# Opening of a fused attention and feed-forward kernel: other load order, two weight quarters centred late, query tiles in spare buffers

## The chip, the cores and the metric

The kernel runs on one core of a Trainium2 chip. The metric is device time in microseconds (us) of one execution; lower is better. The kernel before takes 1200.5 us, the median of three runs (1200.47 to 1202.93).

## The reference

Three blocks follow each other on batches of 576 rows (8 batches, 8 heads of 64, 32 memory slots). Everything is float32 on the host; the matrices w_ch1, w_ch2, w_in and w_out arrive as 64-bit floats.

```
a = softmax(phi over the rows);  k_m = a^T k;  v_m = a^T v
x = softmax(q k_m^T / 8) v_m                      # heads side by side: (8, 576, 512)
xn = (x - mean) / sqrt(var + 1e-6) * g_ln
x = x + relu(xn @ w_ch1) @ w_ch2                  # 512 -> 2048 -> 512
h = gelu(x @ w_in); u, v = halves of h
v = layernorm(v) * g_ln2; v = w_sg @ v + b_sg     # mixes the 576 rows
out = x + (u * v) @ w_out
```

## The kernel before, in words

Phase 1 does attention and the first feed-forward block, phase 2 the rest. Two batches make a pair of nine 128-row tiles; the last 64 rows of both batches share the fifth tile.

W1 (w_ch1) is used in four quarters `fb` of 512 columns. Since x is attn times v_m, the kernel multiplies each quarter by v_m first (`make_vw`, product `pvw`, L561), so that the first feed-forward product `ph` (`m1`, L609) takes the attention weights `aTh`, `aTl` directly. The mean that the layer norm subtracts is taken out of W1 instead: `center_w1` forms the column means of a scaled quarter on TensorE (`cm`, L509; for quarters 1 to 3 in L514 and L521) and subtracts them in place on VectorE (L523), and only then does `make_vw` read the quarter. A matrix product is three products of a high and a low part; `evict_vw` casts the high part on ScalarE (L567) and forms the low part on VectorE (L568).

64-bit weights become 32-bit in `to_f32`: one pass on ScalarE (L116) and two on VectorE (L117, L118) per 128x512 piece. `scale_w1` then scales a W1 piece (L501), `split_w2` splits one of the sixteen W2 pieces.

The hidden layer goes in chunks of 128 columns: `m1` makes `ph` (six products) in one of two PSUM buffers, `relu` takes it out as `hh` on ScalarE (L595) and `hl` on VectorE (L596), and three chunks later `m2` multiplies it by W2 into `py` (L639 to L641). So the third chunk in a row cannot begin before the `hl` of the first is done. A block is 256 or 320 rows; for batch 0 two blocks (j0 and j1) take turns, four chunks each per quarter.

The order is set by `at_time(time, function)`: a sorted list of events, emitted between the chunks. A scheduler then orders each engine's instructions; `issue_after` holds an instruction behind a named one. Every engine works through its own queue in order. All loads and stores go through the one queue of SyncE (SP, `load`, L89) in the order in which they stand there.

For batch 0 phi is loaded, its maximum over the rows subtracted (`prep_max`, `prep_exp`), k_m and v_m formed (`prep_kv`), the query tiles turned (`t_q`), and softmaxed (`t_scores`, `t_norm`, `t_attn`) in three groups: two tiles, two tiles, and the 64 remaining rows. From batch 1 on a query tile lies in one buffer (tag `q`), is turned on VectorE (L381), and the next load waits for that.

Of the kernel before, what the change touches and what calls it, by code (L numbers as in the profile page):

```python
# [28 lines left out]
def fused_kernel(ctx: ExitStack, tc: tile.TileContext, q, k, v, phi, g1, w1, w2, w_in, g2, w_sg, b_sg, w_out, out):  # L29
# [36 lines left out]
    make_identity(nc, ident)  # L66
# [39 lines left out]

    def to_f32(raw, gate=None):
# [4 lines left out]
        gates = ExitStack()  # L112
        for ins in gate or ():
            gates.enter_context(tc.issue_after(ins.ins))
        with gates:
            A.activation(hi.bitcast(F32), hi.bitcast(F32), AF.Prelu, scale=2.0 ** -112, alpha=-(2.0 ** 32))  # L116
            V.tensor_scalar(lo, lo, 29, None, op0=ALU.logical_shift_right)  # L117
            V.scalar_tensor_tensor(out=lo, in0=hi, scalar=3, in1=lo, op0=ALU.logical_shift_left, op1=ALU.bitwise_or)  # L118
        return lo.bitcast(F32)
# [27 lines left out]
    def phase1():  # L147
# [10 lines left out]
        VBs = [[at.tile([P, 2, 4 * D], F32R, name=f"VB{n}{i}") for n in "hl"] for i in range(2)]  # L158
        for i in range(2):
            for t in VBs[i]:  # L160
                G.memset(t.bitcast(F32), 0.0)
        prz = at.tile([P, 2, 4, NM], F32, name="prz")
        G.memset(prz, 0.0)
# [66 lines left out]
        def load_q(u, b, i):  # L230
            n = u["n"]
            if b == 0:
                if i % 2 == 0:
                    t = wpool.tile([P, 2, DM], F32, tag="w", name="q0") if i == 4 else tail.tile([P, 2, DM], F32, tag="vw", name="q0", bufs=VTAIL)
                    st["q0"] = t[:, 0, :], t[:, 1, :]
                t = st["q0"][i % 2].rearrange("p (c o d) -> p c o d", c=4, o=2)[:n]
                load(t.rearrange("p c o d -> p (c o) d"), q[b, :, i * P:i * P + n, :].rearrange("h p d -> p h d"))
            else:
                t = at.tile([P, 4 * DM // 16, 4], F32, tag="q", name="q").rearrange("p a b -> p (a b)")[:, 0:4 * n]
                if n == P:  # L240
                    load(t, u["q_d"].rearrange("a (t r) c f -> (a t) (r c f)", t=32))
                else:
                    for a in range(4):
                        load(t[32 * a:32 * a + 32], u["q_d"][a, 0:n].rearrange("(t r) c f -> t (r c f)", t=32))
            u["q"] = t
            u["seen"].add("q")

        def prep_max(b, gs):
            ph, pr = st["phi", b]
            n, hs = len(gs), slice(4 * gs[0], 4 * gs[-1] + 4)  # L250
            p, tag = (at, "kvn") if gs[0] == 0 else (at, "z")
            pm = p.tile([P, H, NM], F32, tag=tag, name="pm")[:, hs]
            with tc.issue_after(st["hl"].ins) if b else ExitStack():
                V.tensor_reduce(out=pm, in_=ph[:, hs].rearrange("p h c m -> p h m c"), axis=AX.X, op=ALU.max)
                for i, g in enumerate(gs):
                    rows, sub = slice(REM * g, REM * g + REM), slice(4 * i, 4 * i + 4)
                    V.tensor_tensor(out=pm[rows, sub], in0=pm[rows, sub], in1=pr[rows, g], op=ALU.max)
# [107 lines left out]
        def t_q(gr, i):  # L365
# [9 lines left out]
            if b == 0:  # L375
                pt = ps_0([P, 4, n], "ptq")
                for c in range(4):
                    PE.transpose(pt[:, c, :], t[:, c].rearrange("p o d -> p (o d)"), ident[:n, :n])
# [11 lines left out]
        def t_scores(gr):  # L390
# [7 lines left out]
            with whole(b):  # L398
                for kT, cs in parts:
                    for j in range(4):  # L400
                        for g in range(2):
                            rs_, ms = slice(64 * g, 64 * g + 64), slice(32 * j, 32 * j + 32)
                            mm = PE.matmul(sc[g][ms, cs], kT[rs_, ms], qT[rs_, j, cs], start=True, stop=True, skip_group_check=True)  # L403
                            for name in claims:
                                tc.add_manual_dep(mm.ins, name, ORDER, reason="all eight parts of the array together")
            nb = 2 * w // 32
# [4 lines left out]
            for g in range(2):  # L411
                V.transpose(out=z[:, g * w:(g + 1) * w], in_=sc[g])
# [3 lines left out]
            V.tensor_tensor(out=z3, in0=z3, in1=m.unsqueeze(2).to_broadcast([P, nb, NM]), op=ALU.subtract)  # L416
            A.activation(z, z, AF.Exp, scale=SCALE)
            gr["z"] = z, z3, nb

        def t_norm(gr):  # L420
            z, z3, nb = gr["z"]
            r = at.tile([P, 16], F32, tag="r0", name="r0")[:, 0:nb]
            V.tensor_reduce(out=r, in_=z3, axis=AX.X, op=ALU.add)
# [4 lines left out]
        def t_attn(gr):  # L428
# [6 lines left out]
            for i, u in enumerate(us):  # L435
# [6 lines left out]
                A.copy(ah, src)  # L442
# [52 lines left out]
        def scale_w1(fb):  # L495

            WC[fb] = ws = wc_tiles()
            for j, raw in enumerate(raws.pop(fb)):
                d = ws[j // 2][:, j % 2, :]
                w = to_f32(raw, [st.get("hl", tiles[TB - 1]["tr"])] if fb else None)  # L500
                last = A.activation(d, w, AF.Copy, scale=g1c[:, j:j + 1])  # L501
            st["scales"] = [last.ins.name]

        def center_w1(fb):
# [5 lines left out]
            else:  # L510
                four = ps_of(fb, [P, DM], "cm4")
                claim = V.memset(four[:, 0:2], 0.0).ins.name
                for j in range(KC):
                    ins = PE.matmul(four[32 * j:32 * j + 32], mean[:, 0:32], ws[j // 2][:, j % 2, :], start=True, stop=True, skip_group_check=True)  # L514
                    tc.add_manual_dep(ins.ins, claim, ORDER, reason="all four parts of the array together")
                    for other in st["scales"]:
                        tc.add_manual_dep(ins.ins, other, ORDER, reason="all four parts of the array together")
                part = at.tile([P, DM], F32, tag="at32", name="part")
# [3 lines left out]
            for n in range(2):  # L522
                V.tensor_tensor(out=ws[n], in0=ws[n], in1=cm.unsqueeze(1).to_broadcast([P, 2, DM]), op=ALU.subtract)  # L523
# [10 lines left out]
        def make_vw(b, turns):  # L534
# [20 lines left out]
            with whole(b):  # L555
                for fb, ps in runs:
                    ws = WC[fb]
                    for j in range(KC):
                        for g in range(HK):
                            rs_, ms = slice(64 * g, 64 * g + 64), slice(32 * j, 32 * j + 32)  # L560
                            mm = PE.matmul(ps[g][ms, :], vT[rs_, ms], ws[j // 2][rs_, j % 2, :], start=True, stop=True, skip_group_check=True)  # L561
                            for n in claims:
                                tc.add_manual_dep(mm.ins, n, ORDER, reason="all eight parts of the array together")

        def evict_vw(b, turn):
            for ps, (h, l) in zip(st.pop(("vw", b, turn)), VW[b, TURNS[b % 2][turn]]):
                A.copy(h, ps)  # L567
                V.tensor_tensor(out=l, in0=ps, in1=h.bitcast(F32), op=ALU.subtract)  # L568
# [5 lines left out]
        def split_w2(c):  # L574

            gate = st.get("hl", tiles[1 if c == 0 else 3]["tr"])
            W2[c] = split([raws.pop(("w2", c))], wpool, gate=[gate])
# [83 lines left out]

        last_q = -99.0
        for b in range(B):
# [17 lines left out]
            at_time(pb - 2 if b == 0 else pb + 0.6 * f, load_rem, b)  # L681
# [32 lines left out]
            for gi, (items, base) in enumerate(zip(groups, bases)):  # L714
# [6 lines left out]
                if b == 0:  # L721
                    for i, (tt, qi, _, ub) in enumerate(items):
                        at_time(-27, load_q, us[i], ub, qi)
                        at_time(-21 + 0.1 * tt, t_q, gr, i)
                        at_time(1.3 + tt + (tt > 1), t_x, gr, i)
                    tt = items[-1][0]
                    at_time(-17 + 0.1 * tt, t_scores, gr)
                    at_time(-16 + 0.1 * tt, t_norm, gr)
                    at_time(-16 + 0.1 * tt, t_attn, gr)
# [5 lines left out]
                for i, (tt, qi, _, ub) in enumerate(items):  # L735
                    at_time(base - early - 2 + 0.5 * i, lay_q, us[i], ub, qi)
                    at_time(max(base - early, last_q + 0.05), load_q, us[i], ub, qi)
# [18 lines left out]
        for fb in range(NFB):  # L756
            at_time((-26.5, -26.2, -2.5, 2.0)[fb], load_w1, fb)
            at_time((-16.5, -5.0, 3.0, 7.5)[fb], scale_w1, fb)
            at_time((-16.4, -0.3, 4.6, 9.1)[fb], center_w1, fb)
            at_time((-15, 1.3, 5.8, 10.3)[fb], make_vw, 0, [fb])  # L760
            at_time((-15, 1.3, 5.8, 10.3)[fb], evict_vw, 0, fb)
            at_time((1.4, 3.0, 7.4, 12.0)[fb], store_w1, fb)
        for c in range(NF):
            split_at = 4.5 * (c // 4) + 0.5625 * (c % 4) - 0.6 if c > 3 else 0.9 * c - 4
# [383 lines left out]
```

## Time and profile before

| what | value |
|---|---|
| median of three runs | 1200.5 us |
| the profiled execution | 1201.19 us |
| its span in the trace | 1199.4 us |
| TensorE busy over the span | 97% |
| granted TensorE clock, mean | 0.991 of full |

TensorE (PE) is the engine to watch: from about 150 us on it has hardly any idle time. In the rows, DVE is VectorE, ACT is ScalarE, POOL is GpSimd, SP is SyncE, and SPq its queue. Times are us from the start of the span; L numbers are lines of the kernel before.

### The profile page before, as it was taken

The numbers are of one execution on the slowest core, as the hardware profiler recorded it, in microseconds if no ns is written. First come the engines' busy times: TensorE is split into PE (matmuls) and PEld (weight loads), VectorE is DVE, ScalarE is ACT, GpSimd is POOL, SyncE is SP. The second block draws the span as 40 slices with busy tenths as digits, with TensorE's granted clock in tenths as the row PEclk, the third lists the DMA queues.
The fourth block names the chain that finished last, engine by engine and source line by source line (L and its number), as shares of the span: only waits on it lengthen the run. The fifth ranks groups of instructions, "written<-read, shape, count | busy, mean of one in ns | idle before, by whom it ended". The sixth has DMA issues, their size and how long they took to land.

```text
span 1199.4 us, 20678 instructions
## 1 busy us (share of the span) xinstructions
PE 1163.3 (97%) x7717; PEld 988.3 (82%) x7717; DVE 685.6 (57%) x1666; ACT 468.6 (39%) x1066; POOL 401.5 (33%) x623
## 2 busy tenths in 40 slices
PE   4799799999999999999999999999999999999998
PEld 3477578888788888788888888889989988998997
DVE  4896655755644646644546455567575376447532
ACT  3764332323432332422333345445444354344430
POOL 2224221311201211201211112557666476566641
PEclk9799999999999999999999999999999999999999
DMA  8984825463341642241410343122340051022201
GB/s 236 377 250 133 216 74 135 112 181 63 97 126 22 162 115 67 88 117 27 120 36 27 107 140 98 36 74 89 89 141 10 19 158 62 1 88 89 71 19 71
DMA packets 198580, 124.14 MB, mean 104 GB/s; under 512 B 92944, under 2 KB 173712, under 8 KB 198480
## 3 DMA queue, kind: packets, MB, share of 16 engines
q1 hardware_dynamic: 198480, 122.82, 35.8%
q8 instruction: 61, 1.00, 0.3%
q14 instruction: 39, 0.32, 0.1%
HBM read 99.72 MB, written 31.33 MB: 109 GB/s over the span
## 4 chain that ended last, share of the span: by engine, by line
PE 87%; DVE 5%; DMA 3%; SPq 2%; ACT 1%; issue 1%; POOL 1%; POOLq 0%; DVEq 0%
PE ph L609 16%; PE py L639 10%; PE py L641 10%; PE py L640 10%; PE pvs L1053 8%; PE po L1076 8%; PE pv L943 8%; PE pu L1028 7%; PE pvw L561 2%; SPq L89 2%; DMA q<-q_d 2%; PE kvp L317 1%; DVE qT L381 1%; PE sc L403 1%; PE px L460 1%
## 5 line engine op out<-in xcount | busy, mean ns | idle before, releaser
L609 PE MATMUL ph<-aTh,vw 128*128 128x320 f32 (+1 forms) x1024 | 248.4, 301 | 6.9 <-DVE hl L596 4.4
L639 PE MATMUL py<-whl,hh 128*128 128x512 f32 x512 | 201.6, 396 | 4.9 <-ACT hh L595 4.8
L609 PEld LDWEIGHTS ph<-aTh,vw 128*128 128x128 f32 x1024 | 178.9, 190 | 32.5 <-DVE hl L596 8.8
L640 PE MATMUL py<-whl,hh 128*128 128x512 f32 x512 | 201.3, 393 | 0.0
L641 PE MATMUL py<-whl,hl 128*128 128x512 f32 x512 | 182.7, 397 | 0.0
L595 ACT ACTIVATE hh<-ph 128x256 fp32r<-128x256 f32 x256 | 96.8, 386 | 168.1 <-PE ph L609 109.6
L596 DVE SCALAR_TENSOR_TENSOR hl<-ph,hh 128x256 fp32r<-128x256 f32 x256 | 106.6, 421 | 89.1 <-ACT hh L595 88.2
L609 PE MATMUL ph<-aTl,vw 128*128 128x256 f32 (+1 forms) x512 | 152.5, 298 | 0.0
L639 PEld LDWEIGHTS py<-whl,hh 128*128 128x128 f32 x512 | 96.3, 188 | 30.9 <-ACT hh L595 8.1
L1053 PE MATMUL pvs<-wsh,vhl 128*128 128x288 f32 x576 | 121.1, 295 | 0.0
L640 PEld LDWEIGHTS py<-whl,hh 128*128 128x128 f32 x512 | 96.5, 188 | 18.5
L1028 PE MATMUL pu<-yTh,whl 128*128 128x288 f32 x512 | 111.0, 295 | 0.2 <-DVE ug L932 0.2
L609 PEld LDWEIGHTS ph<-aTl,vw 128*128 128x128 f32 x512 | 97.4, 190 | 10.8 <-issue 3.3
L641 PEld LDWEIGHTS py<-whl,hl 128*128 128x128 f32 x512 | 90.2, 189 | 11.6 <-issue 2.1
L1053 PEld LDWEIGHTS pvs<-wsh,vhl 128*128 128x128 f32 x576 | 94.3, 188 | 0.8
L943 PE MATMUL pv<-whl,yTh 128*128 128x512 f32 x288 | 90.8, 395 | 0.0
L1076 PE MATMUL po<-whl,gh 128*128 128x512 f32 x288 | 90.2, 392 | 0.0
L1028 PEld LDWEIGHTS pu<-yTh,whl 128*128 128x128 f32 x512 | 85.1, 188 | 1.9 <-DVE ug L932 0.9
L595 ACT ACTIVATE cr<-ph 128x64 fp32r<-128x64 f32 x128 | 28.7, 227 | 123.1 <-PE ph L609 122.4
L1056 POOL TENSOR_TENSOR gt<-gt,ug 128x288 f32<-128x288 f32 x64 | 52.7, 825 | 68.3 <-DVE gt L1055 61.9
L1053 PE MATMUL pvs<-wsl,vhl 128*128 128x288 f32 x256 | 75.5, 295 | 0.0
L1028 PE MATMUL pu<-yTl,whl 128*128 128x288 f32 x256 | 75.5, 295 | 0.0
(165 smaller groups left out, 2148.9 us busy)
## 6 DMA issues: line engine op xcount, KB each, us to landing
raw<-in_moe_w_ch_dram SPq DMA_DIRECT2D x32, 512.0 KB, 7.9
wc<-w_d SPq DMA_DIRECT2D x28, 512.0 KB, 6.0
y_d<-x SPq DMA_DIRECT2D x36, 256.0 KB, 2.5
yt<-y_d SPq DMA_DIRECT2D x36, 256.0 KB, 2.8
yr<-y_d SPq DMA_DIRECT2D x36, 256.0 KB, 2.9
kv<-in_k_dram SPq DMA_DIRECT2D x32, 256.0 KB, 4.0
kv<-in_v_dram SPq DMA_DIRECT2D x32, 256.0 KB, 4.3
out_dram<-yr SPq DMA_DIRECT2D x32, 256.0 KB, 2.0
```

The lines of the kernel that those rows point to most:

```text
L89: return nc.sync.dma_start(out=out_ap, in_=in_ap)
L595: high = A.activation(out_h, src, AF.Relu)
L596: return high, V.scalar_tensor_tensor(out=out_l, in0=src, scalar=0.0, in1=out_h.bitcast(F32), op0=ALU.max, op1=ALU.subtract)
L609: R["ph"] = PE.matmul(ph, w_[:, ks], x[:, g, 0:w], start=(n == 0), stop=(n == 3 * HK - 1))
L639: PE.matmul(py, hh, wh, start=start, stop=False)
L640: PE.matmul(py, hh, wl, start=False, stop=False)
L641: PE.matmul(py, hl, wh, start=False, stop=stop)
L943: PE.matmul(pv, y[:, kc, cs], w, start=(n == 0), stop=(n == 3 * KC - 1))
L1028: PE.matmul(pu, w[:, ds_], y[:, kc, cs], start=(n == 0), stop=(n == 3 * KC - 1))
L1053: PE.matmul(pvs, v_, w_, start=(n == 0), stop=(n == len(ops) - 1))
L1056: G.tensor_tensor(out=gt, in0=gt, in1=ug, op=ALU.mult)
L1076: PE.matmul(po, gg[:, dc, cs], w, start=(n == 0), stop=(n == 3 * KC - 1))
```

## The change

Loads: the zeroing of `prz` (the rest rows of phi) comes first on GpSimd, and its two loads stand right behind phi; the rest rows of k and v come after all of k and v; only the first two query tiles of batch 0 are loaded ahead of W1's first quarter, the other three behind it. Softmax: batch 0's first group is taken through scores, norm and turning before the second. Means: for quarters 0 and 1 `center_w1` only stores the negative means (`ncm`, ScalarE); `make_vw` adds a second product with them to the uncentred one, and the centring in place (`center_late`) follows later, since the stored quarter is read again by later batches. Gates: the conversion of the next quarter and of W2 pieces is held behind the low parts of the last quarter and behind `center_late`. Queries: in batch 1 every second query tile lies in one of the seven `x` buffers.

```diff
-            with tc.issue_after(st["kvT", b][1].ins):
+            with behind([lead["ah"] if b == 0 else st["kvT", b][1]]):
...
-                w = to_f32(raw, [st.get("hl", tiles[TB - 1]["tr"])] if fb else None)
+                w = to_f32(raw, [st["hl"], *lead["quarter"]] if "hl" in st else [lead["ah"], R["word"]] if fb else None)
...
-                part = at.tile([P, DM], F32, tag="at32", name="part")
+                part = at.tile([P, DM], F32, tag="at32" if fb == 3 else "q", name="part")
...
+            if fb < 2:
+                st["cm", fb] = at.tile([P, DM], F32, tag="at32" if fb else "z", name="ncm")
+                A.mul(st["cm", fb], cm, -1.0)
+                lead["quarter"] = lead["scaled"],
+            else:
+                for n in range(2):
+                    centred = V.tensor_tensor(out=ws[n], in0=ws[n], in1=cm.unsqueeze(1).to_broadcast([P, 2, DM]), op=ALU.subtract)
+                lead["quarter"] = lead["scaled"], centred
+
+        def center_late(fb):
+            with behind([st["hl"], *lead["quarter"]]):
+                for ws in WC[fb]:
+                    centred = V.tensor_tensor(out=ws, in0=ws, in1=st["cm", fb].unsqueeze(1).to_broadcast([P, 2, DM]), op=ALU.add)
+            lead["quarter"] = lead["scaled"], centred
...
+                    if late:
+                        for j in range(KC):
+                            for g in range(HK):
+                                rs_, ms = slice(64 * g, 64 * g + 64), slice(32 * j, 32 * j + 32)
+                                PE.matmul(ps[g][ms, :], vT[rs_, ms], st["cm", fb][rs_], start=False, stop=True, skip_group_check=True)
...
+                if b == 1 and i % 2:
+                    t = mo.tile([P, DM], F32, tag="x", name="q", bufs=7)
...
-            at_time((-16.5, -5.0, 3.0, 7.5)[fb], scale_w1, fb)
+            at_time((-17.5, -5.0, 3.0, 7.5)[fb], scale_w1, fb)
...
+            if fb < 2:
+                at_time((1.6, 6.2)[fb], center_late, fb)
```

VectorE's queue around the low parts of quarter 1, before (`vw` is the low part, `hl` the chunk's low part, `s` the layer-norm statistics of a tile):

```order
L568 TENSOR_TENSOR vw<-pvw,vw 128x512 x2
L469 BN_STATS s_697<-x 128x6
L512 MEMSET cm_796 128x2
L470 BN_AGGR mv<-s_697 128x2
L472 TENSOR_SCALAR ve<-mv 128x2
L95 TENSOR_SCALAR rs_t<-ve 128x2
L469 BN_STATS s_917<-x 128x6
L596 SCALAR_TENSOR_TENSOR hl<-ph,hh 128x256
```

The same place now (line numbers are those of the changed kernel; L597 is the low part, L545 `center_late`, L119 and L120 the conversion, L628 `hl`):

```order
L597 TENSOR_TENSOR vw<-pvw,vw 128x512 x2
L545 TENSOR_TENSOR wc<-wc,ncm 128x1024 x2
L119 TENSOR_SCALAR raw_515<-raw_515 128x512
L119 TENSOR_SCALAR raw_517<-raw_517 128x512
L119 TENSOR_SCALAR raw_519<-raw_519 128x512
L119 TENSOR_SCALAR raw_521<-raw_521 128x512
L481 BN_STATS s_713<-x 128x6
L524 MEMSET cm_812 128x2
L628 SCALAR_TENSOR_TENSOR hl<-ph,hh 128x256
```

Two centring passes and four conversion passes have come to stand between the low parts and the first `hl`.

VectorE's queue around the low parts of quarter 2 now (L279 and L282 subtract phi's maximum for batch 1):

```order
L597 TENSOR_TENSOR vw<-pvw,vw 128x512 x2
L545 TENSOR_TENSOR wc<-wc,ncm 128x1024 x2
L119 TENSOR_SCALAR raw_634<-raw_634 128x512
...
L279 TENSOR_TENSOR phi<-phi,mb 128x1024
L282 TENSOR_TENSOR prz<-prz,mb 64x128 x2
L120 SCALAR_TENSOR_TENSOR raw_634<-raw_634 128x512
L120 SCALAR_TENSOR_TENSOR raw_636<-raw_636 128x512
L120 SCALAR_TENSOR_TENSOR raw_638<-raw_638 128x512
L120 SCALAR_TENSOR_TENSOR raw_640<-raw_640 128x512
L628 SCALAR_TENSOR_TENSOR hl<-ph,hh 128x256
```

Before, the low parts of quarter 2 had one conversion pass between them and then only `cr`, L273 and L276 (as L279 and L282 here) ahead of `hl`; the centring of quarter 1 and all four conversions stood earlier.

TensorE's queue at quarter 1's product, before (`py` is the second feed-forward product, here of block j1, `px` the attention output of a tile):

```order
L561 MATMUL pvw<-wc,kvT 32x512 x8
L639 MATMUL py_760<-whl,hh 128x512
L640 MATMUL py_760<-whl,hh 128x512
L639 MATMUL py_764<-whl,hh 128x512
...
L641 MATMUL py_764<-whl,hl 128x512
L609 MATMUL ph<-aTh,vw 128x256
```

The same place now (L592 is the product with the means, L641 is `ph`, L472 `px`):

```order
L673 MATMUL py_780<-whl,hl 128x512
L585 MATMUL pvw<-wc,kvT 32x512 x8
L592 MATMUL pvw<-ncm,kvT 32x512 x8
L641 MATMUL ph<-aTh,vw 128x256
L641 MATMUL ph<-aTl,vw 128x256
L641 MATMUL ph<-aTh,vw 128x256
L641 MATMUL ph<-aTl,vw 128x256
L472 MATMUL px<-VBh_142,aTl 128x4x64
```

The twelve `py` that stood between the product and the first `ph` of the quarter now stand ahead of the product.

## Rows read from the trace of the kernel before

**Rows 1.** The page, part 1: busy us, share, instructions.

```profile
PE 1163.3 (97%) x7717; PEld 988.3 (82%) x7717; DVE 685.6 (57%) x1666; ACT 468.6 (39%) x1066; POOL 401.5 (33%) x623
```

**Rows 2.** Windows: length, engines busy (x), PEclk, DMA share, GB/s.

```profile
31.05:36.30 5.25, 5.24 (x6) 1.80 (x6) 4.83 (x13) 5.15 (x10) 0.40 (x1) 0.54 1.03 415
40.68:47.24 6.56, 3.15 (x16) 2.22 (x16) 6.56 (x20) 3.41 (x8) 0.85 (x1) 0.92 1.00 400
47.24:53.00 5.76, 5.76 (x23) 3.68 (x24) 4.25 (x9) 4.80 (x10) 2.48 (x2) 0.50 0.88 301
53.00:119.00 66.00, 65.25 (x444) 49.95 (x444) 49.05 (x113) 39.69 (x85) 22.14 (x27) 1.00 0.71 211
119.00:155.00 36.00, 28.44 (x200) 20.62 (x200) 22.82 (x62) 12.79 (x34) 7.57 (x10) 0.95 0.84 229
141.70:145.10 3.40, 3.40 (x10) 3.01 (x11) 2.87 (x9) 1.45 (x3) 0.00 (x0) 0.50 0.91 181
```

**Rows 3.** Windows of the loading stretch, for their last column.

```profile
3.00:7.50 4.50, 0.00 (x0) 0.00 (x0) 1.94 (x2) 0.00 (x0) 0.49 (x2) 1.00 1.00 282
7.50:10.50 3.00, 0.41 (x2) 0.28 (x2) 0.57 (x2) 0.00 (x0) 0.00 (x0) 1.00 0.46 101
16.50:21.00 4.50, 4.35 (x44) 2.83 (x38) 1.22 (x5) 1.18 (x3) 1.08 (x3) 1.00 1.10 194
```

**Rows 4.** Timeline of SP's queue: start, us, what.

```profile
3.98 2.91 SPq L89 DMA_DIRECT2D prz<-in_phi_dram  x2
```

**Rows 5.** Timeline of DVE in the opening.

```profile
9.75 0.60 DVE L257 TENSOR_TENSOR pm<-pm,prz 64x128 f32<-64x128 f32 x2 [4.29 <-DMA prz<-in_phi_dram]
```

**Rows 6.** Timeline of ACT in the opening.

```profile
29.13 0.71 ACT L116 ACTIVATE raw<-raw 128x512 f32<-128x512 f32 x1 [0.62 <-DMA raw<-in_moe_w_ch_dram]
```

**Rows 7.** Timeline of PE in the opening.

```profile
31.05 5.24 PE L509 MATMUL cm<-wc,mcol 128*128 128x512 f32 x6 [1.02 <-ACT wc L501]
...
40.68 0.39 PE L609 MATMUL ph<-aTh,vw 128*128 128x256 f32 x1 [0.88 <-ACT vw L567]
...
47.24 0.58 PE L609 MATMUL ph<-aTh,vw 128*128 128x256 f32 x1 [2.91 <-DVE hl L596]
```

**Rows 8.** Lines of DVE, 62 to 93 us: count, busy us, mean ns.

```profile
L118 DVE SCALAR_TENSOR_TENSOR raw<-raw 128x512 uint32<-128x512 uint32 x13 | 8.5, 688 | 0.1
L596 DVE SCALAR_TENSOR_TENSOR hl<-ph,hh 128x256 fp32r<-128x256 f32 x9 | 3.8, 419 | 0.6 <-ACT hh L595 0.4
L117 DVE TENSOR_SCALAR raw<-raw 128x512 uint32<-128x512 uint32 x9 | 3.5, 421 | 0.0
L469 DVE BATCH_NORM_STATS2 s<-x 128x6 f32<-128x512 f32 x4 | 2.8, 692 | 1.6 <-ACT x L463 1.6
L568 DVE TENSOR_TENSOR vw<-pvw,vw 128x512 fp32r<-128x512 f32 x4 | 2.7, 685 | 0.0
L523 DVE TENSOR_TENSOR wc<-wc,cm 128x1024 f32<-128x1024 f32 x2 | 2.4, 1231 | 0.0
L254 DVE TENSOR_REDUCE pm<-phi 128x256 f32<-128x1024 f32 x1 | 2.0, 2043 | 0.0
L273 DVE TENSOR_TENSOR phi<-phi,mb 128x1024 f32<-128x1024 f32 x1 | 1.2, 1222 | 0.4 <-PE mb L272 0.4
```

**Rows 9.** Timeline of PE at quarter 1's product.

```profile
65.06 1.09 PE L561 MATMUL pvw<-wc,kvT 64*32 64x512 f32 x16
...
68.96 0.28 PE L609 MATMUL ph<-aTh,vw 128*128 128x256 f32 x1
...
71.56 0.40 PE L609 MATMUL ph<-aTh,vw 128*128 128x256 f32 x2
```

**Rows 10.** Timeline of PE, batch 1's queries.

```profile
132.71 0.41 PE L609 MATMUL ph<-aTh,vw 128*128 128x320 f32 x1 [1.46 <-DVE hl L596]
...
141.70 0.79 PE L639 MATMUL py<-whl,hh 128*128 128x512 f32 x1 [3.63 <-ACT hh L595]
```

**Rows 11.** Timeline of DVE, the same stretch.

```profile
138.86 1.08 DVE L381 STREAM_TRANSPOSE qT<-q 128x512 f32<-128x512 f32 x1 [4.27 <-DMA q<-q_d]
```

More of the change, by code (lines that the diff above doesn't have):

```diff
@@ L105, in rsqrt_of, with behind @@
         return y
+    def behind(gate):
+        es = ExitStack()
+        for ins in gate or ():
+            es.enter_context(tc.issue_after(ins.ins))
+        return es
     def to_f32(raw, gate=None):
@@ L110, in to_f32 @@
         lo, hi = words[:, :, 0], words[:, :, 1]
[L112 to L115, printed above, removed]
+        with behind(gate):
             A.activation(hi.bitcast(F32), hi.bitcast(F32), AF.Prelu, scale=2.0 ** -112, alpha=-(2.0 ** 32))
             V.tensor_scalar(lo, lo, 29, None, op0=ALU.logical_shift_right)
-            V.scalar_tensor_tensor(out=lo, in0=hi, scalar=3, in1=lo, op0=ALU.logical_shift_left, op1=ALU.bitwise_or)
+            R["word"] = V.scalar_tensor_tensor(out=lo, in0=hi, scalar=3, in1=lo, op0=ALU.logical_shift_left, op1=ALU.bitwise_or)
         return lo.bitcast(F32)
@@ L158, in phase1 @@
         VBs = [[at.tile([P, 2, 4 * D], F32R, name=f"VB{n}{i}") for n in "hl"] for i in range(2)]
+        prz = at.tile([P, 2, 4, NM], F32, name="prz")
+        G.memset(prz, 0.0)
+        make_identity(nc, ident)
         for i in range(2):
@@ L376, in t_q @@
                 pt = ps_0([P, 4, n], "ptq")
-                for c in range(4):
-                    PE.transpose(pt[:, c, :], t[:, c].rearrange("p o d -> p (o d)"), ident[:n, :n])
+                with behind([lead["sc"]] if "sc" in lead else None):
+                    for c in range(4):
+                        PE.transpose(pt[:, c, :], t[:, c].rearrange("p o d -> p (o d)"), ident[:n, :n])
                 A.copy(out, pt)
@@ L410, in t_scores @@
                 z = at.tile([P, 4 * P], F32, tag="z", name="z")[:, 0:2 * w]
-            for g in range(2):
-                V.transpose(out=z[:, g * w:(g + 1) * w], in_=sc[g])
+            with behind([lead["sub"]] if b == 0 and "sub" in lead else None):
+                for g in range(2):
+                    V.transpose(out=z[:, g * w:(g + 1) * w], in_=sc[g])
             z3 = z.rearrange("p (b m) -> p b m", m=NM)
@@ L422, in t_norm @@
             r = at.tile([P, 16], F32, tag="r0", name="r0")[:, 0:nb]
-            V.tensor_reduce(out=r, in_=z3, axis=AX.X, op=ALU.add)
+            with behind(lead.get("evicted") if gr["b"] == 0 and gr["n"] < P else None):
+                V.tensor_reduce(out=r, in_=z3, axis=AX.X, op=ALU.add)
             V.tensor_scalar(r, r, 1e-9, None, op0=ALU.add)
@@ L514, in center_w1 @@
                     ins = PE.matmul(four[32 * j:32 * j + 32], mean[:, 0:32], ws[j // 2][:, j % 2, :], start=True, stop=True, skip_group_check=True)
-                    tc.add_manual_dep(ins.ins, claim, ORDER, reason="all four parts of the array together")
-                    for other in st["scales"]:
-                        tc.add_manual_dep(ins.ins, other, ORDER, reason="all four parts of the array together")
-                part = at.tile([P, DM], F32, tag="at32", name="part")
+                    for name in (claim, lead["scaled"].ins.name):
+                        tc.add_manual_dep(ins.ins, name, ORDER, reason="all four parts of the array together")
+                part = at.tile([P, DM], F32, tag="at32" if fb == 3 else "q", name="part")
                 A.copy(part, four)
@@ L521, in center_w1 @@
                 PE.matmul(cm, quart.to_broadcast([P, P]), part, start=True, stop=True)
-            for n in range(2):
-                V.tensor_tensor(out=ws[n], in0=ws[n], in1=cm.unsqueeze(1).to_broadcast([P, 2, DM]), op=ALU.subtract)
+            if fb < 2:
+                st["cm", fb] = at.tile([P, DM], F32, tag="at32" if fb else "z", name="ncm")
+                A.mul(st["cm", fb], cm, -1.0)
+                lead["quarter"] = lead["scaled"],
+            else:
+                for n in range(2):
[6 more added lines that the diff above has]
+            lead["quarter"] = lead["scaled"], centred
         def store_w1(fb):
@@ L560, in make_vw @@
                             rs_, ms = slice(64 * g, 64 * g + 64), slice(32 * j, 32 * j + 32)
-                            mm = PE.matmul(ps[g][ms, :], vT[rs_, ms], ws[j // 2][rs_, j % 2, :], start=True, stop=True, skip_group_check=True)
+                            late = b == 0 and fb < 2
+                            mm = PE.matmul(ps[g][ms, :], vT[rs_, ms], ws[j // 2][rs_, j % 2, :], start=True, stop=not late, skip_group_check=True)
                             for n in claims:
                                 tc.add_manual_dep(mm.ins, n, ORDER, reason="all eight parts of the array together")
+                    if late:
[3 more added lines that the diff above has]
+                                PE.matmul(ps[g][ms, :], vT[rs_, ms], st["cm", fb][rs_], start=False, stop=True, skip_group_check=True)
         def evict_vw(b, turn):
             for ps, (h, l) in zip(st.pop(("vw", b, turn)), VW[b, TURNS[b % 2][turn]]):
-                A.copy(h, ps)
-                V.tensor_tensor(out=l, in0=ps, in1=h.bitcast(F32), op=ALU.subtract)
+                high = A.copy(h, ps)
+                low = V.tensor_tensor(out=l, in0=ps, in1=h.bitcast(F32), op=ALU.subtract)
+            lead.setdefault("evicted", (high, low))
+            if b == 0:
+                lead["quarter"] = high, low
         def load_w2(c):
@@ L574, in split_w2 @@
         def split_w2(c):
-            gate = st.get("hl", tiles[1 if c == 0 else 3]["tr"])
-            W2[c] = split([raws.pop(("w2", c))], wpool, gate=[gate])
+            gate = [st["hl"]] if "hl" in st else [*lead["evicted"], tiles[1 if c == 0 else TB]["tr"]]
+            W2[c] = split([raws.pop(("w2", c))], wpool, gate=gate)
         hid, ybank, carry = {}, {}, {}
@@ L660, in phase1 @@
         }
+        lead = {}
         last_q = -99.0
```

44 lines of the change are left out of this document (22 added, 22 removed).

## The prediction

> **What bounds the kernel now.** I read the page's busy times first, then windows of the first 155 us, then the timelines of each engine with their waits, then the groups by line. TensorE is busy 97% of the span, VectorE 57%, ScalarE 39% [rows 1], so TensorE is the bound, and the change can give or take time only where TensorE idles or runs at a low clock, or where it gets more work. The windows show where that is. From 53 to 119 us TensorE is busy 65.25 of 66.0 us at full clock: quarters 1 to 3 of batch 0 run there without a gap. Before it, 40.68 to 47.24 has 3.15 busy of 6.56, and the 5.76 us after it run at a granted clock of 0.50, the lower of the two levels (1.2 GHz). From 119 to 155, where batch 1 begins, 28.44 of 36.0 are busy [rows 2]. So there are two places to gain: the opening, and batch 1's queries. And there is a stretch between them with nothing to gain and everything to lose. There VectorE is busy 49.05 of 66.0 us [rows 2], 74%, the second busiest engine.
>
> All sums go against the profiled execution, 1201.19 us (span 1199.4 and 1.8 around it); the median of the runs is 0.7 lower, which I take off at the end.
>
> **The change part by part.**
>
> *A, the first `ph` of the program: -1.9 us.* SP's queue now waits 2.91 us at the `prz` loads, behind the zeroing [rows 4], and the DMA moves only 101 GB/s from 7.5 to 10.5 us, against 282 before [rows 3]. With the zeroing first, that stretch runs at 282: 3.0 us x (1 - 101/282) = 1.9 us. Moving three query tiles (two of 128 rows and one of 64, 512 floats each: 0.66 MB) behind W1's first quarter, at the 194 GB/s at which query tiles come now [rows 3], takes another 3.3 us from ahead of it. Its last piece reaches ScalarE at 29.13 after a wait on the DMA [rows 6] and would come at about 23.9. That `prz` itself is there earlier is worth little: VectorE waited 4.29 us for it [rows 5], but k and v come behind it. The 5.2 us are not all kept. The three query tiles now land at about 27, and in the new order the second group's turning and scores stand ahead of the column means on TensorE, some 2.5 us of products and copies. Then all eight `cm` records run in one go: six take 5.24 us, 0.87 each, at a clock of 0.54 [rows 2, 7], so eight take 7.0 and end at about 36.6. Storing the negative means is one ScalarE pass, 0.6; the second product (C) 1.1, partly beside it; the first cast 0.88 [rows 7]. The first `ph` then starts at 38.8 instead of 40.68. Bounds: -5.3 if all 5.2 us come through, 0 if the moved queries eat them all.
>
> *B, the rest of the opening: -1.2 us.* From 40.68 to 53.0 there are 3.4 us idle before the third chunk, 2.91 of them one wait for the first `hl`, and a low clock over 5.76 us, worth half of it, 2.9 [rows 2, 7]: 6.3 with nothing else. The two in-place centrings (1.23 each [rows 8]) leave VectorE here, which brings the first `hl` earlier, but ScalarE has casts of the second group and two W2 conversions queued at the same place. I give it half of the 2.46, 1.2. Bounds: -4 (the idle and a little of the clock go) and +1.5 (the second W2 piece becomes late).
>
> *C, the second product of quarter 1: +1.1 us.* Sixteen small products, as many as the sixteen `pvw` that take 1.09 [rows 9]. Quarter 0's is in A. Bounds 0.5 and 1.5.
>
> *D, the seam at quarter 1: +6.7 us.* Before, the product stands ahead of twelve `py`, 2.8 us of other work in which the cast and the low parts are made, and the centring was done long before [rows 9]. Now the `py` come first, so TensorE waits for the cast, 0.9. And on VectorE the first `hl` stands behind: two low parts 1.37, two centrings 2.46, four conversion passes at 0.42, one statistic 0.69, `hl` itself 0.42 [rows 8]. With the cast that is 7.5 us from the product's end. TensorE has until then the first two chunks with two tiles' `px`, which took 3.0 us before (68.96 to 71.96, [rows 9]), and four `py` at 0.235 (2.8/12), 0.94: 3.9. The third chunk needs the PSUM buffer that `hl` frees: 3.6 us idle, the cast included. Up to the third `hl` come five more passes at 0.69, two at 0.42 and two `hl`, 5.1 us, against two chunks of 1.7 (six `ph` at 0.12 and four `py`): 1.7 idle. Before the fourth stand the maxima of batch 1's phi, 2.04 together, a pass and `hl`, 3.15 against 1.7: 1.4 idle. Sum 6.7. Bounds: 0.9 (only the cast is waited for) and 9.
>
> *E, ahead of quarter 2's product: +1.5 us.* TensorE turns the maxima (`pt`) directly ahead of the product. The product's bank is zeroed on VectorE only after the reduction of `pt` and two passes on `dg`, and a turning of the rest query whose load waits, on SP, for the buffer that `part` now holds; behind that load on SP stand batch 1's further loads. Three small VectorE passes between two TensorE instructions are about 1.5; bounds 0 (the zeroing is not late) and 4 (the query tile is as late as those of rows 11).
>
> *F, the seam at quarter 2: +7.9 us.* As D, with longer work ahead of the first `hl`: cast 0.9, low parts 1.37, centrings 2.46, four passes at 0.42, the subtraction from phi 1.22 and its rest 0.3, four passes at 0.69, `hl` 0.42 [rows 8]: 11.1. TensorE has 12 `ph`, six `px` and `mb` at 0.12 and four `py`, 3.2, so 7.9; the chunks behind need no further wait. Bounds 0.9 and 9.
>
> *G, the clock behind these gaps: +1.7 us.* Behind the 3.63 us wait at 141.7, TensorE ran 3.40 us at 0.50 [rows 2, 10], 1.7 lost. I count that once, behind the longest gap. Bounds 0 and 5 (behind D, E and F).
>
> *H, batch 1's queries: -6.0 us.* VectorE waits for a query tile, 4.27 us at 138.86 [rows 11], and in the same way at one more tile ahead of it; TensorE waits behind it 1.46 and 3.63 [rows 10], and loses the 1.7 of clock: 6.8. With every second tile in one of the seven `x` buffers, two tiles are loaded ahead, and batch 0 keeps five. The waits go; two turnings (1.08 each, [rows 11]) now stand ahead of `hl` at quarter 3, and I charge 0.8 for them. Bounds -8 and -3 (the `x` buffers come free late, and one wait stays).
>
> That the kernel's later batches read an already centred quarter 0 and 1 is as before: nothing.
>
> Sum: -1.9 - 1.2 + 1.1 + 6.7 + 1.5 + 7.9 + 1.7 - 6.0 = +9.8; 1201.2 + 9.8 - 0.7 = **1210 us**.
>
> VectorE waits 2.91 us of TensorE's time at 47.24, where one `hl` stands late in its queue [rows 7], which is the mechanism of D and F. The Trainium skill, "PSUM — Partial Sum Buffer", section Engine vs sequencer instructions, says that ScalarE's and VectorE's queues are strict first in, first out. By that no `hl` can pass the centrings in front of it; if it could, D and F would shrink to the casts.
>
> **The rivals.**
>
> *A', faster: the seams hold.* VectorE is idle for 17 of the 66 us from 53 to 119, and the conversions would only trade places within that slack: what D and F put ahead of `hl` is no longer done earlier. If at each seam TensorE waits for the cast alone (0.9), the sum is -1.9 - 1.2 + 1.1 + 1.8 - 6.0 = -6.2: 1194. For it speaks the slack; against it that slack elsewhere doesn't help a buffer that is needed now, and that two `ph` buffers give 3 to 4 us of cover. The parts that don't depend on the seams sum to -8.0, so it decides where D to G together cost under 8.0 of their 17.8. The Trainium skill, "Perfetto Trace Analysis", section Identifying the Most-Contended Engine, takes occupancy as a fair measure for VectorE. By that rule VectorE, at 57% and 74% [rows 1, 2], has room for the moved passes and the result is this rival's 1194. The wait at 47.24 shows that a share of busy time doesn't bind at a seam. Chance 0.28.
>
> *B', the opening gives more.* If the column means run at full clock, 0.43 each, the first `ph` starts at 35.4: 3.4 more, 1206.5. For it: the earlier load. Against it: every row of that stretch before is at about half clock [rows 2]. Chance 0.12.
>
> *C', the seams cost more, or the query waits stay.* The low clock follows all three gaps (+3.4), or the `x` buffers come free only after batch 0's tiles and H is nothing (+6.0): about 1215. For it: seven `x` buffers are what they were, with two more users. Chance 0.15.
>
> **How the numbers follow.** Forecast 0.45, with a range of its own of 1204 to 1214. Range 1194 to 1217: from A' to the sum with H gone and G once more. About 0.2% (2.4 us) is what a measurement of this kernel can tell from no change, 1198.1 to 1202.9. Of A', 0.24 is faster and 0.04 within; of B', 0.01 faster and 0.02 within; all else is slower: faster 0.25, same 0.06, slower 0.69.
>
> **What would show it.** A: the last piece of W1's first quarter reaches ScalarE at about 24, and the first `ph` starts near 38.8. B: the wait for the first `hl` of the program is under 2.9. D and F: in the 53 to 119 us stretch TensorE has 12 to 17 us idle, as waits of 2 to 7 us for `hl` right behind the two products of quarters 1 and 2, with the centrings running on VectorE at that time. E: a wait for the zeroing at quarter 2's product. G: a granted clock near 0.5 behind the longest gap. H: no wait over 1 us for a query tile in batch 1. I am wrong if the seams show waits of about 1 us, as A' says, or if VectorE runs the centrings beside other TensorE work.

## The result

The changed kernel takes 1217.11 us (median, 1216.58 to 1217.88) against 1200.52: ratio 1.0131, 95% interval [1.0117, 1.0145]. That is slower, as forecast, by 16.6 us where 9.5 were forecast, and 0.1 us over the upper end of the range. The profiled execution's span is 1216.1 us against 1199.4.

The two stretches of [rows 2] with the same bounds, in the changed kernel (windows: length, then PE, PEld, DVE, ACT, POOL busy, PEclk, DMA share, GB/s):

```profile
53.00:119.00 66.00, 49.52 (x268) 36.80 (x267) 43.20 (x96) 35.83 (x72) 15.43 (x21) 0.85 0.64 189
119.00:155.00 36.00, 34.51 (x270) 25.04 (x269) 21.28 (x56) 13.82 (x35) 10.37 (x12) 0.95 0.60 162
```

TensorE lost 15.7 us of busy time where it had been saturated, and what it ran there ran at a mean clock of 0.85. In the second stretch it idles 1.5 us instead of 7.6.

TensorE's waits, from the timeline (start, length, what, and in brackets the idle time and what ended it). `ph` is L641 now, `pvw` L585, the product with the means L592, `hl` L628, the high part's cast L596:

```profile
39.35 0.39 PE L641 MATMUL ph<-aTh,vw 128*128 128x256 f32 x1 [0.74 <-ACT vw L596]
...
42.77 0.74 PE L671 MATMUL py<-whl,hh 128*128 128x512 f32 x2 [1.47 <-ACT hh L627]
...
47.89 0.73 PE L671 MATMUL py<-whl,hh 128*128 128x512 f32 x2 [2.02 <-ACT whl L132]
...
65.33 1.09 PE L585 MATMUL pvw<-wc,kvT 64*32 64x512 f32 x16
66.21 1.06 PE L592 MATMUL pvw<-ncm,kvT 64*32 64x512 f32 x16
68.01 0.39 PE L641 MATMUL ph<-aTh,vw 128*128 128x256 f32 x1 [0.73 <-ACT vw L596]
...
72.09 0.50 PE L671 MATMUL py<-whl,hh 128*128 128x512 f32 x1 [0.73 <-ACT hh L627]
...
73.93 0.39 PE L641 MATMUL ph<-aTh,vw 128*128 128x256 f32 x1 [0.64 <-DVE hl L628]
...
78.33 0.41 PE L641 MATMUL ph<-aTh,vw 128*128 128x320 f32 x1 [0.86 <-DVE hl L628]
...
81.17 0.42 PE L641 MATMUL ph<-aTh,vw 128*128 128x320 f32 x1 [1.70 <-DVE hl L628]
...
101.11 1.09 PE L585 MATMUL pvw<-wc,kvT 64*32 64x512 f32 x16 [2.16 <-DVE pvw L575]
106.91 0.58 PE L641 MATMUL ph<-aTh,vw 128*128 128x256 f32 x1 [4.71 <-ACT vw L596]
...
117.54 0.58 PE L641 MATMUL ph<-aTh,vw 128*128 128x256 f32 x1 [3.85 <-DVE hl L628]
```

At the two seams TensorE waits for casts and for `hl`, as D and F said, though at quarter 1 no single wait for `hl` is over 1.70 us; at quarter 2 two more waits, 2.16 and 4.71 us, stand around the product, where E had 1.5 in all. Behind both groups of waits the clock is at the lower level. Windows there, columns as above:

```profile
81.90:88.70 6.80, 6.21 (x18) 5.05 (x18) 1.79 (x8) 6.01 (x12) 2.29 (x6) 0.50 0.34 98
101.11:106.91 5.80, 1.09 (x16) 0.19 (x16) 0.03 (x2) 1.17 (x3) 2.30 (x6) 0.60 0.87 275
106.91:117.54 10.63, 6.26 (x24) 5.27 (x24) 10.54 (x17) 6.41 (x12) 3.29 (x3) 0.66 0.64 183
117.54:120.50 2.96, 2.96 (x10) 2.67 (x11) 2.51 (x5) 1.25 (x4) 1.34 (x4) 0.50 0.64 100
120.50:123.49 2.99, 2.99 (x12) 2.36 (x11) 0.42 (x1) 0.57 (x2) 2.42 (x2) 0.62 0.97 225
```

What holds `hl` at quarter 2 is read from VectorE's timeline. `hh`, which `hl` needs, starts on ScalarE at 112.07 (two in 0.65 us); `hl` starts at 117.06, behind this:

```profile
106.89 1.29 DVE L597 TENSOR_TENSOR vw<-pvw,vw 128x512 fp32r<-128x512 f32 x2 [5.77 <-ACT vw L596]
108.10 2.35 DVE L545 TENSOR_TENSOR wc<-wc,ncm 128x1024 f32<-128x1024 f32 x2
110.36 1.43 DVE L119 TENSOR_SCALAR raw<-raw 128x512 uint32<-128x512 uint32 x4
111.71 1.22 DVE L279 TENSOR_TENSOR phi<-phi,mb 128x1024 f32<-128x1024 f32 x1
112.84 0.59 DVE L282 TENSOR_TENSOR prz<-prz,mb 64x128 f32<-64x128 f32 x2
113.46 3.57 DVE L120 SCALAR_TENSOR_TENSOR raw<-raw 128x512 uint32<-128x512 uint32 x4
117.06 0.42 DVE L628 SCALAR_TENSOR_TENSOR hl<-ph,hh 128x256 fp32r<-128x256 f32 x1
```

These are the passes of F's working, in its order (the four of L120 took 3.57 us where 2.76 were counted, the rest a little less): VectorE doesn't idle from 106.89 on, and `hl` waits 4.3 us in its queue though both `hh` are done at 112.72.

The 2.16 us ahead of the product are VectorE's too: between the turned maxima (`pt`, done on TensorE at 98.96) and the second zeroing of the product's bank (L575, 101.00) stand a conversion pass of 1.18 us from 98.89 on and then the small passes that E counted.

The 4.71 us ahead of the first `ph` are another thing. ScalarE's queue, then what SP's queue waited for between 84 and 112 us (in total, times, longest):

```profile
105.74 0.65 ACT L118 ACTIVATE raw<-raw 128x512 f32<-128x512 f32 x1 [4.92 <-DMA raw<-in_moe_w_ch_dram]
106.29 1.06 ACT L596 CAST vw<-pvw 128x512 fp32r<-128x512 f32 x2
```

```profile
SPq L88 <- ACT wc L513: 9.7, 2, 8.2
SPq L88 <- PE cm L532: 7.2, 1, 7.2
```

The casts stand behind the conversion of a W1 piece whose load is late; that load stands on SP behind loads that wait, 8.2 us for the scaling that frees a raw buffer and 7.2 for the column mean that frees `part`.

### The profile page after: what moved, and what is told of

The parts are those of the page before. It is cut to its first block, busy times and chain, and to the rows that moved or that the text cites. A ratio compares the mean times of both kernels' runs of the same rounds, so it can differ in the third digit from the quotient of the medians.

```text
span 1216.1 us, 20762 instructions
## 1 busy us (share of the span) xinstructions
PE 1172.3 (96%) x7749; PEld 993.1 (82%) x7749; DVE 691.7 (57%) x1673; ACT 470.2 (39%) x1068; POOL 401.3 (33%) x623
## 4 chain that ended last, share of the span: by engine, by line
PE 86%; DVE 6%; DMA 3%; ACT 2%; SPq 1%; issue 1%; POOL 1%; POOLq 0%; ACTq 0%; DVEq 0%
PE ph L641 16%; PE py L671 10%; PE py L673 10%; PE py L672 10%; PE pvs L1088 8%; PE po L1111 8%; PE pv L978 8%; PE pu L1063 7%; PE pvw L585 2%; SPq L88 1%; PE kvp L323 1%; DVE raw L120 1%; PE sc L410 1%; DMA q<-in_q_dram 1%; PE px L472 1%
## 5 line engine op out<-in xcount | busy, mean ns | idle before, releaser
L641 PE MATMUL ph<-aTh,vw 128*128 128x320 f32 (+1 forms) x1024 | 250.0, 303 | 15.2 <-DVE hl L628 8.4
L641 PEld LDWEIGHTS ph<-aTh,vw 128*128 128x128 f32 x1024 | 180.1, 192 | 43.7 <-DVE hl L628 11.5
L628 DVE SCALAR_TENSOR_TENSOR hl<-ph,hh 128x256 fp32r<-128x256 f32 x256 | 106.5, 421 | 100.7 <-ACT hh L627 99.8
L641 PE MATMUL ph<-aTl,vw 128*128 128x256 f32 (+1 forms) x512 | 153.2, 300 | 0.0
L641 PEld LDWEIGHTS ph<-aTl,vw 128*128 128x128 f32 x512 | 98.1, 192 | 9.7 <-issue 2.5
```

Source lines behind the costliest of these rows:

```text
L628: return high, V.scalar_tensor_tensor(out=out_l, in0=src, scalar=0.0, in1=out_h.bitcast(F32), op0=ALU.max, op1=ALU.subtract)
L641: R["ph"] = PE.matmul(ph, w_[:, ks], x[:, g, 0:w], start=(n == 0), stop=(n == 3 * HK - 1))
```

## The experiments

Ratios are to the kernel before, measured beside it on the same chip, with 95% intervals. The changed kernel's, 1.0131, was measured at another time; a difference of two ratios is turned to us with 1200, and by their intervals it is good to about 2 to 3 us.

**e1, `part` elsewhere.**

```diff
-part = at.tile([P, DM], F32, tag="at32" if fb == 3 else "q", name="part")
+part = at.tile(..., tag="at32", ...) if fb == 3 else wpool.tile([P, DM], F32, tag="w", name="part")
```

> The changed kernel, but `part` of quarters 1 and 2 lies in a weight buffer instead of the query buffer, so that the rest query's load need not wait for the column means. Theory (the query load that waits 7.2 us on SP holds the W1 load behind it, whose conversion on ScalarE stands ahead of quarter 2's casts): the waits of TensorE at quarter 2's product, 2.16 and 4.71 us, fall to about 1 us each or less, and the time falls by 4 to 9 us, the clock behind them included. Rival (the W1 load is late because its buffers come free late, after quarter 2's scaling): the cast is still waited for over 3 us and the time falls by under 2 us.

Measured: 1.0084 [1.0064, 1.0104], so 5.6 us less than the changed kernel. At quarter 2's product, TensorE's timeline of e1:

```profile
101.15 1.09 PE L585 MATMUL pvw<-wc,kvT 64*32 64x512 f32 x16
104.92 0.39 PE L641 MATMUL ph<-aTh,vw 128*128 128x256 f32 x1 [2.68 <-ACT vw L596]
```

The wait ahead of the product is gone and the cast's is 2.0 shorter, not under 1: the W1 piece is still late (ScalarE waits 4.08 us for it). So `part`'s buffer costs about what the theory said. The rest of that wait isn't shown to be the rival's: SP waits here for GpSimd (2.4 us ahead of the last weight load, at 100.54) and, for an earlier one, 2.7 us for the column mean that frees `part`, which now holds a weight buffer, not for quarter 2's scaling.

**e2, the conversion's gate.**

```diff
-w = to_f32(raw, [st["hl"], *lead["quarter"]] if "hl" in st else ...)
+w = to_f32(raw, [st["hl"]] if "hl" in st else ...)
```

> The changed kernel, but a W1 quarter's conversion is held behind the last `hl` alone, no longer behind the low parts and the late centring. Theory (VectorE's queue ahead of `hl` is what TensorE waits for at the two seams): the conversion passes move ahead of the low parts; of the 4.5 us idle at quarter 1's seam about 1.5 are left (centrings 2.35, low parts 1.3, statistic 0.7, hl 0.4 and the cast 0.7 make 5.5 against 3.9 of cover), of the 4.4 at quarter 2's at most 2.5, the low clock behind the first goes (3.1): 5 to 10 us less. Rival (the centrings alone are enough to hold hl): under 3 us less.

Measured: 1.0064 [1.0044, 1.0083], 8.0 us less. The waits at the seams in e2:

```profile
72.70 0.50 PE L671 MATMUL py<-whl,hh 128*128 128x512 f32 x1 [0.73 <-ACT hh L627]
...
78.90 0.42 PE L641 MATMUL ph<-aTh,vw 128*128 128x320 f32 x1 [0.86 <-DVE hl L628]
...
98.05 1.96 PE L585 MATMUL pvw<-wc,kvT 64*32 64x512 f32 x16 [1.91 <-DVE pvw L575]
...
100.74 0.58 PE L641 MATMUL ph<-aTh,vw 128*128 128x256 f32 x1 [0.73 <-ACT vw L596]
...
105.79 0.50 PE L671 MATMUL py<-whl,hh 128*128 128x512 f32 x1 [0.72 <-ACT hh L627]
```

With the conversions no longer between the low parts and `hl`, `hl` is hardly late at either seam though the centrings stay ahead of it: 1.6 us left at quarter 1 of 4.5 behind the cast, and the 3.85 of quarter 2 gone. The centrings alone don't hold it. The wait for the zeroing ahead of quarter 2's product stays, 1.91 us. And the cast is waited for 0.73 us only: the last of the four weight loads that SP issues here leaves by 94.6 us, in the changed kernel at 102.67.

**e3, quarters 0 and 1 centred in place again,** the rest as changed.

```diff
-            if fb < 2:
+            if fb < 0:
                 st["cm", fb] = at.tile(...)
...
-                            late = b == 0 and fb < 2
+                            late = False
```

(and `center_late` is not called).

> The changed kernel, but quarters 0 and 1 are centred in place ahead of their product as in the kernel before, without the second product; the gates, the load order and the query buffers stay as changed. Theory: 2.35 us leave the queue ahead of `hl` at either seam, but the four first and four second conversion passes stay, so the seams lose about 2 us each and TensorE 2.1 us of work, while the centring stands ahead of the product: 3 to 7 us less than the changed kernel. Rival (the late centring is the whole loss): 15 us less or more, at or under the kernel before.

Measured: 1.0023 [1.0010, 1.0035], 13.0 us less: far over my 3 to 7, and nearer to the rival's 15 than to them. TensorE at quarter 2 in e3:

```profile
93.51 1.09 PE L585 MATMUL pvw<-wc,kvT 64*32 64x512 f32 x16
96.36 0.39 PE L641 MATMUL ph<-aTh,vw 128*128 128x256 f32 x1 [0.18 <-ACT vw L596]
...
104.71 0.50 PE L641 MATMUL ph<-aTh,vw 128*128 128x256 f32 x1 [3.11 <-DVE hl L628]
```

The product waits for nothing and the first `ph` hardly for its cast, with `part` in the query buffer as in the changed kernel: without the late centring in the chain of gates the W1 load is in time. I had counted the queue ahead of `hl` and not what the late centring holds back through the gate. At quarter 2 the wait for `hl`, with eight conversion passes ahead of it, stayed, as expected. At quarter 1 it did not: the eight passes stand ahead of `hl` there too, but TensorE, which ran at the lower clock from 70.9 to 74.0 us, waits only 0.71 for the cast and 0.73 for `hh` (and 1.12 ahead of the product). So at quarter 1 neither the centrings (e2) nor the conversions (here) are enough alone, and at quarter 2 the conversions are.

**e4, the queries alone,** on the kernel before.

```diff
+                if b == 1 and i % 2:
+                    t = mo.tile([P, DM], F32, tag="x", name="q", bufs=7)
...
-at_time(max(base - early, last_q + 0.05), load_q, us[i], ub, qi)
+at_time(base - early + 0.3 if b == 1 and i else max(base - early, last_q + 0.05), load_q, us[i], ub, qi)
```

> The kernel before with only the query part of the change: in batch 1 every second query tile in one of the seven x buffers, loaded earlier. Theory (the 1.46 and 3.63 us waits and the low clock at 130 to 145 us go): 5 to 8 us less than the kernel before. Rival (what batch 1 gains here shows only because the changed kernel reaches it 20 us later, when the loads are done anyway): under 2 us less.

Measured: 0.9977 [0.9962, 0.9992], 2.8 us less, between the two. Both waits of [rows 10] are gone, but this one is new:

```profile
156.63 1.09 PE L564 MATMUL pvw<-wc,kvT 64*32 64x512 f32 x16 [2.63 <-DMA wc<-w_d]
```

A stored W1 quarter, which nothing waited for before, is now late. In the traces e4 is still 5.2 us ahead at this product (156.63 against 161.83), so the wait doesn't account for all that is missing from the 5 to 8.

**e5, everything but the late centring, its gate and `part`'s buffer** (e3, with e2's edit and `part` in its old buffer).

> The changed kernel with quarters 0 and 1 centred in place again, the conversion held behind the last hl alone, and part in its old buffer: what is left of the change is the load order, the first softmax and the query buffers. Theory (all of the loss between 68 and 123 us comes from the late centring, the gate tied to it and part's buffer; the opening gives about 3, the queries about 7, of which a new wait for a stored W1 quarter takes some back): 5 to 9 us under the kernel before. Rival (the new opening itself hurts the stretch that follows): not faster than the kernel before.

Measured: 0.9970 [0.9959, 0.9981], 3.6 us less than before; 5 to 9 were expected, and by the rival none.

**e6, the same without the query buffers:** only the new opening (load order, first softmax, and the gates and times of the first W2 pieces).

> As the last one, without the query buffers: only the load order, the zeroing first and the order of the first softmax are changed against the kernel before. Theory: 1 to 4 us under the kernel before (1.3 from the earlier first ph and 1.5 from the rest of the opening). Rival (the opening is moved and nothing else; what comes earlier waits for the second W2 piece): 0 to 2 us over it.

Measured: 1.0034 [1.0021, 1.0047], 4.1 us more than before: not the theory, and more than the rival's 0 to 2. So the new opening costs time in this order of work, and the queries give back 7.7 (1.0034 to 0.9970). TensorE in e6:

```profile
49.37 0.73 PE L671 MATMUL py<-whl,hh 128*128 128x512 f32 x2 [2.79 <-ACT whl L132]
...
67.85 1.09 PE L585 MATMUL pvw<-wc,kvT 64*32 64x512 f32 x16 [0.37 <-ACT wc L513]
70.26 0.39 PE L641 MATMUL ph<-aTh,vw 128*128 128x256 f32 x1 [1.32 <-ACT vw L596]
```

The wait for the first `hl` in [rows 7] (2.91) has become one for the second W2 piece (2.79), and `ph` of quarter 1 waits for its cast with no `py` behind the product, here too, without any late centring. Most of the cost shows only later: in the two traces e6 is 0.6 us ahead at the first `ph`, 1.3 behind at quarter 1's (70.26 against 68.96), 3.0 at quarter 2's product (88.95 against 85.95) and 4.6 at quarter 3's (121.92 against 117.35). Between them lie `ph` at the lower clock behind the cast's wait (0.93 from 70 to 95 us, before 1.00) and a wait of 1.15 for `hl`.

**e7, e1 and e2 together;** the late centring stays.

> The changed kernel with both things beside the late centring undone: conversion held behind the last hl alone, and part in a weight buffer. The late centring, its second product and the place of the twelve py stay. Theory: the two savings (about 6 and 8 us) overlap in the clock behind them and sum to 10 to 13, so 3 to 6 us over the kernel before, and at the two seams TensorE waits 2 to 3 us each. Rival (the centring passes in VectorE's queue are the main loss): under 9 us less than the changed kernel.

Measured: 1.0025 [1.0015, 1.0035], 12.7 us less than the changed kernel, 3.0 over before: as the theory said. What separates it from e5 (1.0025 against 0.9970, 6.6 us) is the late centring with its second product, with nothing held behind it, and `part` in a weight buffer; the two weren't taken apart.

**e8, the queries and `prz` first,** the rest of the opening as before (e4, with the zeroing moved and `load_rem` at `pb - 0.5`).

> The kernel before with the query buffers and, of the new opening, only the zeroing of prz first and its loads ahead of k and v (rest rows of k and v last); query tiles, softmax order and W2 conversions as before. Theory: the stretch of 101 GB/s at 7.5 us goes, W1's last piece comes about 2 us earlier and so does the first ph; 1 to 2 us under the run with the query buffers alone (0.9977 of before), so about 0.996 to 0.997. Rival (the earlier ph meets the same later waits): 0.9977 again.

Measured: 0.9974 [0.9959, 0.9989], the same as e4; the interval takes in the theory's 0.996 to 0.997 too. The traces speak for the rival: the first `ph` comes 0.6 us earlier than in e4 (39.88 against 40.51), not 2, and at quarter 2's product both are at 85.84. The earlier loads alone are worth nothing that shows.

**e9, e5 with the W2 pieces of the opening as before.**

```diff
-gate = [st["hl"]] if "hl" in st else [*lead["evicted"], tiles[1 if c == 0 else TB]["tr"]]
+gate = [st["hl"]] if "hl" in st else [tiles[1 if c == 0 else 3]["tr"]]
...
-... else 0.1 * c - 6 if c else -16.0
+... else 0.9 * c - 4
```

> The last-but-one combination (new opening and query buffers, centring in place, conversion behind hl alone; 0.997 of before), with the W2 pieces of the opening converted at the times and behind the gates of the kernel before, ahead of or between quarter 0's first chunks. Theory (the new opening loses its gain to the second W2 piece: 2.84 us wait for its cast): that wait goes, 1 to 4 us less. Rival (the W2 work on ScalarE and VectorE now comes ahead of the casts and hl of quarter 0, so the first ph is later): no gain.

Measured: 0.9974 [0.9962, 0.9985]: no gain over e5, the rival. The wait for the second W2 piece is gone, but the first `ph` comes at 43.36 us, in e5 at 39.28.

**e10, e5 with only that gate changed.**

```diff
-... else [*lead["evicted"], tiles[1 if c == 0 else TB]["tr"]]
+... else [*lead["evicted"], tiles[1 if c == 0 else 3]["tr"]]
```

> The same combination, with only the gate of the opening's W2 pieces changed from the last tile's softmax to the fourth's, their times as changed. Theory: the second W2 piece's cast comes ahead of the fifth tile's work on ScalarE, the 2.84 us wait falls under 1, and 1 to 3 us go. Rival: TensorE waits for hl or hh instead, no gain.

Measured: 0.9959 [0.9945, 0.9974], 4.9 us under the kernel before, the lowest ratio here; from e5 it isn't told apart by the intervals. TensorE in e10:

```profile
44.11 1.22 PE L671 MATMUL py<-whl,hh 128*128 128x512 f32 x2 [1.08 <-ACT whl L132]
...
52.79 0.50 PE L671 MATMUL py<-whl,hh 128*128 128x512 f32 x1 [2.04 <-ACT hh L627]
...
67.43 1.09 PE L585 MATMUL pvw<-wc,kvT 64*32 64x512 f32 x16 [0.50 <-ACT wc L513]
68.45 0.51 PE L671 MATMUL py<-whl,hh 128*128 128x512 f32 x1
```

The W2 wait went from 2.84 to 1.08 and a wait for `hh` of 2.04 came: within the opening little is won. But `py` stand behind quarter 1's product again and cover the cast.

## Why the prediction was right or wrong

The direction, the places and the mechanism of the two seams were right; the size was short by 7 us. E and G together were 11.1 us too low, D and F 4.3 too high, so part of the miss cancelled. The upper end of the range, the sum with H gone and G once more, works out to 1218.0 and not to the 1217 that was stated. Term by term, forecast and measured, from the two traces:

| term | forecast | measured | from |
|---|---|---|---|
| A first `ph` | -1.9 | -1.3 | 39.35 against 40.68 |
| B rest of the opening | -1.2 | -1.2 | `ph` of quarter 1 at 68.01 against 68.96, less A, C and the cast's 0.73 |
| C second product | +1.1 | +0.9 | 65.33 to 66.21 |
| D seam at quarter 1 | +6.7 | +5.2 | the cast's 0.73, and 4.5 idle from 68.01 to 88.70 |
| E ahead of quarter 2's product | +1.5 | +6.1 | 2.16, and 4.71 less 0.73 |
| F seam at quarter 2 | +7.9 | +5.1 | 0.73, and 4.37 idle from 106.91 to 117.54 |
| G clock | +1.7 | +8.2 | estimate: TensorE's busy time times (1 - PEclk) in the five windows above: 3.1, 0.4, 2.1, 1.5, 1.1 |
| H queries | -6.0 | -7.5 | from the next `pvw` (149.40, before 125.61) to the fourth behind (178.11, before 161.83) |
| sum | +9.8 | +15.5 | the spans differ by 16.7 |

A's loads came as worked out: the last piece of W1's first quarter is on ScalarE by 24, and the eight `cm` start at 29.75, where the working has 29.6. The rest is two errors against each other. The `cm` took 5.81 us, not 7.0: the first five start 0.85 us apart, the last three 0.43, which is the pace of B'; so B' came true for three of eight. And from their end to the first `ph` it took 3.8 us, not 2.2, because the two products of quarter 0 take 3.0 us there.

D and F were sized by the right queue. D's sign, waits of 2 to 7 us for `hl`, came at quarter 2 only (3.85); at quarter 1 they were 0.64, 0.86 and 1.70, and e2 and e3 show that there it took the centrings and the conversions together. F's idle time is 2.8 short of the forecast because the work beside it took TensorE 6.26 us where I had 3.2: by PEclk 2.1 of that is the lower clock, which stands in G, and the rest is work that F had counted too small. `hl` itself came as worked out, 11.2 us from the cast's start (106.29 to 117.48) where I had 11.1. VectorE works strictly in order, as the Trainium skill, "PSUM — Partial Sum Buffer", section Engine vs sequencer instructions, says, and the trace agrees: 4.3 us of `hl` with its input ready. A', the rival by VectorE's share of busy time, is refuted: VectorE was busy 43.2 of the 66 us, less than before, and TensorE idled 16.5.

The steps that failed are E and G. E named both parts of the chain (`part`'s buffer and the loads queued on SP behind it) and then priced only three small VectorE passes, with 4 as its bound: 6.1 were measured. The conversion pass among them (1.18), the W1 load behind the waits on SP, ScalarE's conversion behind that load and the casts behind the conversion were not followed. e1 shows the buffer's share, e2 and e3 the gate's and the late centring's: e1 shortens the wait that the late load makes at quarter 2's cast (4.71 to 2.68 us), e2 and e3 take it away (0.73 and 0.18). They are not additive by single causes: e1 and e2 give 5.6 and 8.0 and together 12.7, while e3 alone gives 13.0. G was counted once, behind the longest gap, with 5 as its bound; the clock fell behind both groups of waits, as C' had it, and 8.2 were lost. Where the waits are shorter, in e7, the clock is 1.00 from 70 to 95 us and 0.93 from 95 to 119, against 0.86 and 0.72 in the changed kernel. That the clock follows these waits is read from such windows; no run changed the clock by itself.

B's number came out, but not by its mechanism. The centrings that it takes off VectorE there ran at 36.33 us before, ahead of the first `ph` and outside its stretch. The first `hl` is in time now, but waits of 1.47 for `hh` and 2.02 for the second W2 piece have come in its place, and TensorE idles 4.3 us from the first `ph` to 53.0, before 3.4. What pays is the clock, 1.00 there against 0.72, to which B gave nothing; e5 and e6 have the same opening and show 1.00 and 0.90 from 40 to 53 us, so this part is luck. By e6 the new opening costs 4.1 us in all: its order puts all twelve `py` ahead of quarter 1's product and the second W2 piece late. The prediction credited the opening with 3.1 (A and B) and counted the lost cover in D without asking which part of the change costs it. Which of the opening's edits moves the `py` is not settled; e10 brings some back with one gate.

H held: the waits of [rows 10] are gone in the changed kernel. That e4 keeps only 2.8 us goes in part with a transfer that was hidden while TensorE waited: the stored quarter's load, 2.63 us late. In e5 the same product starts 1.1 us later, at 157.71, and finds it there; from e6 to e5 the queries are worth 7.7. What else e4 loses stays open.

## What to carry to other kernels

Work that is moved off one path is paid where it lands: look up what the instruction that frees a buffer is queued behind, on its own engine's queue, and count the latency there, not the engine's share of busy time. When a wait is added, follow it through every queue in turn, the DMA queue and the conversion behind the load as well, until something that the bounding engine needs; here waits of 8.2 and 7.2 us in SP's queue ended as 4.71 us on TensorE. And price a gap on TensorE with the clock behind it: here the 11 us of gaps around quarter 2 came with some 5 us lost at the lower clock.

## What was not expected of the hardware

The granted clock of a window says nothing where the trace has no entry for it yet. By its row, the stretch of the eight `cm` products in the changed kernel, 29.75 to 35.56 us, ran at 1.00; but the first entry of the clock in that trace lies at 34.04, and up to there 1.00 stands for want of one. The products tell it themselves: their starts are 0.85 us apart up to 33.32 and 0.43 apart from 34.11 on. Those are the paces of the two levels: before, at 0.50, the starts from 32.07 to 35.48 are 0.85 apart, and in e10 they go from 0.85 to 0.43 at about 31.9 us, where the entry goes from 0.50 to 1.00. `ph` follows the clock too: 256 columns follow each other every 0.12 us at 1.00 and every 0.21 at 0.50 (from 70.9 to 74.0 us in e3). So at the start of a trace the clock is better read from the pace of a product whose pace at both levels is known.
